# Spectral filter times token mixer: the middle stage's instructions fixed in an order written by hand, and the collecting transfers moved to ScalarE's queue

## The chip, the cores and the metric

The kernel runs on one core of one Trainium2 chip. The metric is the device time of one execution in microseconds (us). The core has a matrix engine (TensorE, PE in the profile, with its weight loads as PEld), VectorE (DVE), ScalarE (ACT), GpSimd (POOL) and SyncE (SP), which here only issues transfers. Transfers issued by SP, ScalarE and GpSimd run on 16 DMA engines that they share. An engine works through its instructions in the order in which the program holds them.

## What is computed

The input x has 2,048 rows (the sequence) of 512 channels. All is float32.

```python
xn = layernorm(x)                                  # over the 512 channels
X  = rfft2(xn, axes=(sequence, channels))          # 2048 x 257, complex
s  = irfft2(X * (w_r + 1j * w_i), s=(2048, 512))   # the spectral filter
h  = layernorm(xn)
u  = gelu(einsum("bsd,sf->bdf", h, w1) + b1)       # mixes along the sequence, F = 1792
y  = einsum("bdf,fs->bds", u, w2) + b2             # and back, w2 is 1792 x 2048
out = x + s * silu(y.transpose(0, 2, 1))
```

## The kernel before

**Two chains of work.** The sequence is laid out as 16 rows `j` of 128 partitions. The filter transforms along the sequence in two steps, along the channels in between, multiplies by the weights, and goes the same way back; all transforms are matrix products with constant tables. The mixer needs products of float32 accuracy from a faster number format: each operand is cut into a high part (a rounded copy, made on ScalarE) and a low part (the difference, on VectorE), and each product is three: high with high, high with low, low with high. A *unit* of the mixer's first product (`hidden`, lines 245 to 250) is three such products of 128x128 by 128x512.

**Stage 1 (lines 350 to 432)** goes over the 16 rows: layer norm, the first seven of the 14 column blocks of w1 in PSUM banks 0 to 6, and the first transform of the filter in bank 7, whose result VectorE folds by symmetry into `ey` (`fold`, line 219).

**Stage 2, the middle stage (lines 435 to 687)**, is where the change lies. It does the other seven column blocks in two batches over 16 rows (`hidden_rest`, 32 parts of w1, 4 units each in the first batch, 3 in the second), and beside them the filter in four *quads* (`filter_quad`). A quad is: 64 products along the channels with `ey` (line 476), four copies to `eys` (478), 64 small products that end the transform along the sequence (485), two copies out of banks 4 to 7 with a swap of neighbouring partitions by two transfers on ScalarE's queue each (`swapped`, 495 to 497), eleven VectorE operations in each of two halves that apply the weights (`weighted`, 512 to 522), 64 small products back (538), and four copies (541). The swapped copies have four buffers, so two halves can be in work. Also in this stage: gelu of finished blocks (line 275, three buffers `u`), and for each pair of blocks the *forms*, the sums and differences that the last stage multiplies, cut in high and low parts (`forms`, 287 to 312). The gelu of a bank must be done before a new block can use the bank. Of w1's low parts, some are made by VectorE (`direct`, line 118), others by a ScalarE copy of the negative and an adding transfer from GpSimd (563 to 567). Weights of the filter are loaded by SP into two buffers, each when the product with the one before it is done (`load_weights`, 438); one of the eight is patched with a second transfer, a GpSimd and a VectorE operation (444 to 447).

**Stage 3 (lines 690 to 900)** multiplies the forms by w2 with a scheme of seven products per pair of rows (`ORDER`, line 692), 21 products of 128x256 each (line 863), whose w2 forms are cut on ScalarE and VectorE (710, 711; three buffers). Beside them the filter's result is taken back along the sequence: `gathered` (781) collects one row of `eys` into a tile `yj` by eight transfers, `sequence` (790) and `channels` (799) transform it, and `finish` multiplies and adds. Tiles of stage 3 (`fin`, line 774) lie where the gelu tiles and the w1 parts of stage 2 lay, and each waits for the ones under it.

**What sets the order.** Most instructions are given to a planner, which orders those of one engine by its own estimate of when each can run. `keep` (line 159) holds the instructions passed through it in the order of the program. In stage 1 nearly all of VectorE's and ScalarE's are kept; in the middle stage only TensorE's products are kept, and VectorE, ScalarE and SP go by the planner. The order of TensorE is a script at the end of the stage (lines 633 to 686), where `products(n)` takes n units and `step(n)` one step of quad n. From line 755 the forms and the w2 forms are kept again for the seam to stage 3.

Of the kernel before, what the change touches and what calls it, by code (L numbers as in the profile page):

```python
# [8 lines left out]
F32 = mybir.dt.float32  # L9
# [99 lines left out]

def spectral_mixer_kernel(tc, x, w1, b1, w2, b2, wk, we, wx, c_f, c_ft, c_d, c_i, c_g, c_h, c_s, out):  # L110
    nc = tc.nc
    V, A, G, T, SY = nc.vector, nc.scalar, nc.gpsimd, nc.tensor, nc.sync
# [12 lines left out]
    with tc.tile_pool(name="ps", bufs=1, space=PSUM) as psp, ExitStack() as left, ExitStack() as right:  # L125
# [32 lines left out]

        keep = tc.keep_in_program_order
# [153 lines left out]

        def form_parts(n, i):
            t, k = form[i][n]
            return t[:, k, :D // 2], t[:, k, D // 2:]
# [56 lines left out]
        of.update({2: (m, 0), 3: (m, 1)})  # L373
        folds = iter(())
        for j in range(NJ):
# [54 lines left out]
            folds = fold(j, first_copy(j, z))  # L430
        run(folds)
        rstage.close()
# [5 lines left out]
        def load_weights(k, i):  # L438
# [4 lines left out]
            if at == ends:  # L443
                SY.dma_start(w[:2, 0], wx[:, 0:3:2])
                one, two = w[:2, 0, 1 - i], w[:2, 0, i]
                G.tensor_sub(one, one, two)
                V.scalar_tensor_tensor(two, two, 2.0, one, op0=ALU.mult, op1=ALU.add)
# [21 lines left out]
        def filter_quad(n, los):  # L469

            gf = mp.tile([P, 4, 32], F32, name=f"gf{n}", tag="gf")
            SY.dma_start(gf, c_g[n].rearrange("p (q c) -> p q c", c=32))
            for q, lo in enumerate(los):
                pd = ps[:, 7 - q]
                for b in range(4):
                    keep(T.matmul(pd[:, b * P:(b + 1) * P], ey[:, lo, b].rearrange("p h j -> p (h j)"), cd[:, b],
                                  start=True, stop=True))
                A.activation(eys[:, lo].rearrange("p (s g c) -> p g s c", s=2, c=64),
                             pd.rearrange("p (g s c) -> p g s c", s=2, c=64), AF.Copy)
                if q % 2:  # L480
                    yield

            for q, lo in enumerate(los):
                for hi in range(4):
                    keep(T.matmul(ps[32 * q:32 * q + 32, 4 + hi], gf[32 * hi:32 * hi + 32, q],
                                  eys[32 * hi:32 * hi + 32, lo], start=True, stop=True))
            hf = mp.tile([P, 4, 2, 32], F32, name=f"hf{n}", tag="hf")
            SY.dma_start(hf, c_h[n].rearrange("p (q s c) -> p q s c", s=2, c=32))
            back, half = [], []

            def swapped(h):
                if not places:
                    place(n)
                e, z = places.pop(0), places.pop(0)
                A.activation(e, ps[:, 4 + 2 * h:6 + 2 * h].rearrange("p b (s c) -> p b s c", s=2), AF.Copy)
                A.dma_start(z[0::2], e[1::2])
                A.dma_start(z[1::2], e[0::2])
                half.append((e, z))

            def weighted(h):  # L500
                at = 4 * n + 2 * h
                e, z = half[h]
                wa, wb = (weights[2 * n + h, i] for i in range(2))
                if at == ends:
                    G.memset(z[:2, 0], 0.0)
                pq = mp.tile([P, 2, 2, 256], F32, name=f"pq{n}_{h}", tag="pq")
                s1 = mp.tile([P, 2, 2, 2], F32, name=f"s1_{n}_{h}", tag="s1")
                er, ei, zr, zi, pr, pi = (a[:, :, s] for a in (e, z, pq) for s in range(2))
                G.tensor_mul(s1[:, 0], z[:, :, :, 0], e1[:, at:at + 2])
                G.tensor_mul(s1[:, 1], e[:, :, :, 0], e2[:, at:at + 2])  # L510
                G.tensor_add(s1[:, 0], s1[:, 0], s1[:, 1])
                V.scalar_tensor_tensor(pr, zi, sg[:, 0:1], er, op0=ALU.mult, op1=ALU.add)
                V.scalar_tensor_tensor(pi, zr, sg[:, 0:1], ei, op0=ALU.mult, op1=ALU.subtract)
# [424 lines left out]
```

## Time and profile before

| | us |
|---|---|
| median of three runs | 416.3 (415.81 to 416.79) |
| the profiled execution | 419.44 |
| its span on the core | 417.4 |
| mean granted TensorE clock in it | 0.963 of full speed |

In the profiled execution the first product of stage 1 on real data starts at 6.8, the first line-476 product of the middle stage at 97.8, the first line-863 product of stage 3 at 223.4. Times of rows count from the start of the span. A view of waits lists, for an engine and line, what released it and for how long it stood; a row of the time order has start, duration, engine, line, operation, `out<-in`, shape, and in square brackets the idle time of the engine ahead of it with what ended it. `SPq` and `ACTq` are the queues in which SP and ScalarE issue transfers. In the chain of waits, each row is a piece of the path followed back from the last instruction: start, length, engine, output tile, line and how many instructions.

### The profile page before, as it was taken

Reading aid. Unit: us, or ns where it says so; the run is one execution under the profiler, and the core shown is the slowest. Engines: PE = TensorE matmul, PEld = TensorE weight load, DVE = VectorE, ACT = ScalarE, POOL = GpSimd, SP = SyncE. Lnnn points to the kernel's source line nnn. Section 1 sums busy time; section 2 is a strip of 40 time slices with the busy share of each in tenths; the row PEclk is TensorE's granted clock in tenths of the full one; section 3 lists DMA queues with packets and bytes.
Section 4 is the critical chain, followed back from the end, with each engine's and each line's share of the span. In section 5 each row is a group of like instructions: output and inputs, shape, how many; then the busy total and the mean of one; then the engine's idle time right before and its main releaser. Section 6 shows DMA issues by size and latency. Waiting matters only on the chain.

```text
span 417.4 us, 7663 instructions
## 1 busy us (share of the span) xinstructions
PE 382.1 (92%) x2760; PEld 336.6 (81%) x2760; DVE 307.4 (74%) x654; ACT 217.0 (52%) x389; POOL 85.9 (21%) x130
## 2 busy tenths in 40 slices
PE   8999999999499799996798589999999998979995
PEld 5888888887287577775577579999999898979994
DVE  5899998773698594969968718767676767664774
ACT  4677755658554545453364724545455444533551
POOL 2133332322141683030000001111111111110200
PEclk9999999999689999999699869999999999999999
DMA  8857384118377998774384489999889999797802
GB/s 266 288 163 244 113 295 156 55 36 236 107 178 191 238 244 258 213 235 133 97 239 90 91 134 195 251 191 213 166 214 197 219 184 202 185 186 168 149 7 53
DMA packets 45298, 73.87 MB, mean 177 GB/s; under 512 B 6388, under 2 KB 28668, under 8 KB 45132
## 3 DMA queue, kind: packets, MB, share of 16 engines
q1 hardware_dynamic: 37228, 55.29, 46.7%
q0 software_dynamic: 6752, 13.90, 20.2%
q10 hardware_dynamic: 1280, 4.20, 2.7%
q8 instruction: 21, 0.34, 0.3%
q14 instruction: 17, 0.14, 0.1%
HBM read 60.78 MB, written 8.13 MB: 165 GB/s over the span
## 4 chain that ended last, share of the span: by engine, by line
PE 60%; DVE 13%; DMA 11%; SPq 5%; ACT 4%; issue 4%; POOL 2%; ACTq 0%; DVEq 0%; POOLq 0%
PE ps L863 22%; PE ps L343 18%; DMA yj<-ey 5%; SPq L784 4%; PE ps L211 3%; PE ps L790 3%; DMA w1s<-in_w_dram 3%; PE ps L248 2%; PE ps L250 2%; DMA w1l<-in_w_dram 2%; PE ps L249 2%; DVE w2f L711 2%; PE ps L799 2%; ACT w2f L710 2%; PE ps L332 1%
## 5 line engine op out<-in xcount | busy, mean ns | idle before, releaser
L343 PE MATMUL ps<-h,w1h 128*128 128x512 f32 x224 | 58.5, 398 | 0.0
L250 PE MATMUL ps<-h,w1l 128*128 128x512 f32 x112 | 45.5, 406 | 9.2 <-DVE w1l L118 6.6
L248 PE MATMUL ps<-h,w1h 128*128 128x512 f32 x112 | 47.0, 419 | 4.1 <-ACT u L275 4.1
L343 PEld LDWEIGHTS ps<-h,w1h 128*128 128x128 f32 x224 | 40.9, 188 | 7.9
L863 PE MATMUL ps<-fa,w2f 128*128 128x256 f32 x336 | 47.0, 296 | 0.0
L711 DVE TENSOR_TENSOR w2f<-s,w2f 128x896 fp32r<-128x896 f32 x32 | 34.8, 1091 | 15.1 <-ACT w2f L710 13.9
L249 PE MATMUL ps<-h,w1h 128*128 128x512 f32 x112 | 45.1, 403 | 0.0
L863 PEld LDWEIGHTS ps<-fa,w2f 128*128 128x128 f32 x336 | 44.3, 203 | 0.0
L863 PE MATMUL ps<-fb,w2f 128*128 128x256 f32 x336 | 43.3, 282 | 0.6 <-DVE c L828 0.6
L863 PE MATMUL ps<-fc,w2f 128*128 128x256 f32 x336 | 41.8, 280 | 0.0
L863 PEld LDWEIGHTS ps<-fb,w2f 128*128 128x128 f32 x336 | 40.8, 188 | 1.2 <-issue 0.8
L863 PEld LDWEIGHTS ps<-fc,w2f 128*128 128x128 f32 x336 | 40.4, 188 | 0.0
L710 ACT ACTIVATE w2f<-s 128x896 fp32r<-128x896 f32 x32 | 30.2, 947 | 15.7 <-DVE s L724 6.4
L711 DVE TENSOR_TENSOR w2f<-a,w2f 128x896 fp32r<-128x896 f32 x24 | 26.1, 1089 | 15.6 <-ACT w2f L710 13.5
L701 POOL DMA_DIRECT2D s<-in_w_dram x16 | 13.6, 852 | 102.3 <-DMA s<-in_w_dram 74.2
L250 PEld LDWEIGHTS ps<-h,w1l 128*128 128x128 f32 x112 | 22.0, 196 | 15.6 <-DVE w1l L118 7.0
L710 ACT ACTIVATE w2f<-a 128x896 fp32r<-128x896 f32 x24 | 22.8, 950 | 21.5 <-PE ps L863 18.7
L248 PEld LDWEIGHTS ps<-h,w1h 128*128 128x128 f32 x112 | 22.0, 196 | 13.9 <-issue 5.0
L343 PE MATMUL ps<-h,w1l 128*128 128x512 f32 x112 | 30.6, 389 | 0.0
L790 PE MATMUL ps<-cft,yj 128*128 128x128 f32 x128 | 18.3, 288 | 11.7 <-DMA yj<-ey 10.1
L834 POOL DMA_DIRECT2D out_dram<-g x15 | 12.8, 856 | 75.6 <-DVE g L832 75.5
L118 ACT ACTIVATE w1h<-w1s 128x384 fp32r<-128x384 f32 (+1 forms) x24 | 13.2, 562 | 26.6 <-DMA w1s<-in_w_dram 16.6
(122 smaller groups left out, 739.6 us busy)
## 6 DMA issues: line engine op xcount, KB each, us to landing
a<-in_w_dram SPq DMA_DIRECT2D x24, 448.0 KB, 4.7
s<-in_w_dram POOLq DMA_DIRECT2D x17, 448.0 KB, 6.9
s<-in_w_dram SPq DMA_DIRECT2D x15, 448.0 KB, 3.9
w1s<-in_w_dram SPq DMA_DIRECT2D x48, 128.0 KB, 3.3
w1r<-in_w_dram SPq DMA_DIRECT2D x16, 256.0 KB, 3.3
wa<-in_wk_dram SPq DMA_DIRECT2D x8, 512.0 KB, 4.1
wb<-in_wk_dram SPq DMA_DIRECT2D x8, 512.0 KB, 5.2
ez<-ez ACTq DMA_DIRECT2D x16, 256.0 KB, 3.6
```

The costliest lines, as they stand in the source:

```text
L118: return A.activation(hi, src, AF.Copy), V.tensor_sub(lo, src, hi.bitcast(F32))
L248: keep(T.matmul(o, w[0][:, sl], hh[j], start=first, stop=False))
L249: keep(T.matmul(o, w[0][:, sl], hl[j], start=False, stop=False))
L250: keep(T.matmul(o, w[1][:, sl], hh[j], start=False, stop=last))
L343: T.matmul(ps[:, bank + i], w[wi][:, i * P:(i + 1) * P], hj, start=first and j == 0, stop=last and j == NJ - 1)
L701: G.dma_start(t, w2_half(*added), accum_op=ALU.add)
L710: ordered(A.activation(wf[:, 0], v, AF.Copy))
L711: ordered(V.tensor_sub(wf[:, 1], v, wf[:, 0].bitcast(F32)))
L784: SY.dma_start(yj[16 * r:16 * r + 16], eys[16 * r + j:16 * r + j + 1])
L790: in_turn(j, T.matmul(pf[:, b], yj[:, b * P:(b + 1) * P], cft, start=True, stop=True))
L834: G.dma_start(out[:, j, cols], g[:, cols], accum_op=ALU.add)
L863: in_turn(j0, T.matmul(o, wf[:, wi, i], ui, start=m + a == 0 and n in (1, 2, 5), stop=m == NH - 1 and a == 2, skip_group_check=n in (6, 3, ...
```

## The change

1. *Program order.* Calls of VectorE, ScalarE, TensorE and SP go through a wrapper `InOrder`. From the second to last row of stage 1 to the end of the middle stage its switch is on, and each of their instructions is kept in the order of the program. GpSimd's stay with the planner.
2. *The order written out.* `filter_quad` is cut into `along_channels`, `turned_in`, `forward`, `swapped`, `weighted` (a generator that yields after each VectorE operation), `way_back` and `turned_back`, and a new script places them among the units: `go(units, ops)` takes units and, spread over them, VectorE operations of the filter. The low part of a w1 part comes one unit behind its high part (`later`). Forms are made by `forms_apart`, whose steps give ScalarE's copies first and VectorE's differences one step later. The next weights are loaded right after the product with the ones before.
3. *The start.* The first three w1 parts are loaded a row ahead, and the first two are cut, between gelus, around the last fold. For the first two rows, the three units of banks 2, 0 and 1 come ahead of those of bank 3.
4. *The collecting transfers* are issued by ScalarE; the first two rows' are placed ahead of stage 3's loop, and a few tiles are allocated ahead of them, so that the `yj` tiles lie further back in the pool. These, and stage 3 as a whole, are not in the fixed order.

The arithmetic is the same. The diff, cut to its core:

```diff
+class InOrder:
+    def __init__(self, engine, keep, switch):
+        self.engine, self.keep, self.switch = engine, keep, switch
+    def __getattr__(self, name):
+        call = getattr(self.engine, name)
+        return (lambda *a, **k: self.keep(call(*a, **k))) if self.switch else call
...
-    V, A, G, T, SY = nc.vector, nc.scalar, nc.gpsimd, nc.tensor, nc.sync
+    keep, fixed = tc.keep_in_program_order, []
+    V, A, T, SY = (InOrder(e, keep, fixed) for e in (nc.vector, nc.scalar, nc.tensor, nc.sync))
+    G = nc.gpsimd
...
+        def forms_apart(i):
...
+            first = (d[0], d[1], u[:, 2]), (a, slice(0, 2), u[:, 0:2])
+            highs(*first)
+            yield
+            lows(*first)
+            V.tensor_sub(u[:, 1], u[:, 1], u[:, 3])
+            V.tensor_sub(u[:, 3], u[:, 2], u[:, 3])
+            V.scalar_tensor_tensor(u[:, 2], u[:, 1], -1.0, u[:, 2], op0=ALU.mult, op1=ALU.subtract)
+            V.scalar_tensor_tensor(u[:, 0], u[:, 2], -1.0, u[:, 0], op0=ALU.mult, op1=ALU.subtract)
...
+            yield
...
+            second = (c, slice(0, 2), u[:, 2:4]), (b, slice(0, 2), u[:, 0:2])
+            highs(*second)
+            yield
+            lows(*second)
             yield
...
             folds = fold(j, first_copy(j, z))
+            if j == NJ - 2:
+                fixed.append(True)
+                for i in range(3):
+                    w1_raw(i)
+        gelu(2, 2)
+        w1_part(0, True, False)
+        gelu(0, 0)
         run(folds)
+        w1_part(1, True, True)
+        gelu(1, 1)
         rstage.close()
...
+                V.scalar_tensor_tensor(pr, zi, sg[:, 0:1], er, op0=ALU.mult, op1=ALU.add)
+                yield
                 V.scalar_tensor_tensor(pi, zr, sg[:, 0:1], ei, op0=ALU.mult, op1=ALU.subtract)
-                V.tensor_mul(pq, pq, wa)
+                yield
+                ends_too(k, 0)
+                V.tensor_mul(pq, pq, weights[k, 0])
+                if k < 7:
+                    load_weights(k + 1, 0)
+                yield
...
+        def next_part(i):
+            if i + 3 < len(parts_):
+                w1_part(i + 3, i % 3 == 0 or i + 3 >= NJ, True)
+            if i + 5 < len(parts_):
+                w1_raw(i + 5)
...
+        def go(units, ops=0):
+            for k in range(units):
                 next(rest)
+                while later:
+                    later.pop(0)()
+                for _ in range((k + 1) * ops // units - k * ops // units):
+                    next(work)
+
+        todo.extend(forms_apart(i) for i in FORMS[:3])
         waiting = [[(3, 3)]]
+        load_tables(0)
+        gelu(9, 6)
+        gelu(8, 5)
+        w1_part(2, True, True)
+        gelu(7, 4)
...
+        go(2)
+        along_channels(0, (3, 2))
+        form_step()
+        turned_in(0, (3, 2))
+        form_step()
+        go(2)
+        along_channels(0, (1, 0))
+        form_step()
+        turned_in(0, (1, 0))
+        form_step()
+        go(1)
+        forward(0)
+        swapped(0, 0)
+        form_step()
+        swapped(0, 1)
+        form_step()
+        load_tables(1)
+        go(3)
...
+        go(11, 12)
+        for n in range(1, 4):
+            if n > 1:
+                go(4, 4)
+                along_channels(n, (0, 1))
+                turned_in(n, (0, 1))
+                go(4, 6)
+                along_channels(n, (2, 3))
+                turned_in(n, (2, 3))
+                go(2, 2)
+            forward(n)
+            swapped(n, 0)
+            go(5, 8)
+            swapped(n, 1)
             form_step()
+            go(2)
             form_step()
+            way_back(n - 1)
...
+            go(1)
+            turned_back(n - 1)
+        for k in range(30):
+            go(1)
+            if k < 24:
+                for _ in range((k + 1) * 5 // 6 - k * 5 // 6):
+                    next(work)
+            if k > 4:
+                form_step()
+        run(work)
+        way_back(3)
+        go(1)
+        turned_back(3)
+        go(2)
+        fixed.clear()
         rstage.close()
...
-                SY.dma_start(yj[16 * r:16 * r + 16], eys[16 * r + j:16 * r + j + 1])
+                A.dma_start(yj[16 * r:16 * r + 16], eys[16 * r + j:16 * r + j + 1])
...
+        made = {"p1_0": fp.tile([P, HD], F32, name="p1_0", tag="p1")}
+        gs = [fp.tile([P, D], F32, name=f"g{j}", tag="g", bufs=2) for j in (0, NP)]
+        made["c11_0"] = fp.tile([P, HD], F32, name="c11_0", tag="c", bufs=2)
+        ya, yb = gathered(0), gathered(NP)
         for p in range(NP):
...
-                if k == 0 and p == 0:
-                    ya, yb = gathered(j0), gathered(j1)
```

More of the change, by code (lines that the diff above doesn't have):

```diff
@@ L506, in weighted, with swapped @@
+        def swapped(n, h):
+            if not places:
+                place(n)
+            e, z = half[n, h] = places.pop(0), places.pop(0)
+            A.activation(e, ps[:, 4 + 2 * h:6 + 2 * h].rearrange("p b (s c) -> p b s c", s=2), AF.Copy)
+            A.dma_start(z[0::2], e[1::2])
+            A.dma_start(z[1::2], e[0::2])
+        def weighted(n):
+            for h in range(2):
+                at, k = 4 * n + 2 * h, 2 * n + h
+                e, z = half[n, h]
                 pq = mp.tile([P, 2, 2, 256], F32, name=f"pq{n}_{h}", tag="pq")
@@ new lines, in unit @@
+        def unit(i, k, bank):
+            j = parts_[i][0]
+            hidden(j, k, bank, parts[i])
+        def next_part(i):
[3 more added lines that the diff above has]
+                w1_raw(i + 5)
+            if i >= NJ:
+                passed[0] = i - NJ + 1
+        def hidden_rest():
+            first, second = BATCHES[0][1], BATCHES[1][1]
+            for i in range(2):
+                for k, bank in first[:3]:
+                    unit(i, k, bank)
+                    yield
+            for i in range(2):
+                unit(i, *first[3])
+                next_part(i)
+                yield
+            for i in range(2, NJ):
+                for k, bank in first:
+                    unit(i, k, bank)
+                    if i == NJ - 1 and k != 1:
+                        gelu(*{2: (10, 0), 3: (11, 1), 0: (4, 3)}[k])
+                    if k == 0:
+                        next_part(i)
+                    yield
+            todo.extend([forms_apart(3), forms_apart(4)])
+            waiting.append([(5, 2)])
+            for i in range(NJ, 2 * NJ - LATE // 3):
+                for k, bank in second:
+                    unit(i, k, bank)
+                    if k == 0:
+                        next_part(i)
+                    yield
+            w1_part(2 * NJ - 1, True, False)
@@ L621, in hidden_rest @@
                 gelu(ft, bank)
-        chain = [filter_quad(n, los) for n, los in enumerate(QUADS)]
         rest = hidden_rest()
-        def products(n):
-            for _ in range(n):
+        work = (None for n in range(4) for _ in weighted(n))
+        def go(units, ops=0):
+            for k in range(units):
                 next(rest)
-        def step(n):
-            next(chain[n])
-        for ft, bank in ((9, 6), (8, 5), (7, 4)):
-            gelu(ft, bank)
-        todo.extend(forms(i) for i in FORMS[:3])
```

255 lines of the change are left out of this document (106 added, 149 removed).

## The prediction

> **What bounds the kernel now.** I read the page first, then the chain of waits, TensorE's busy time and granted clock by stretches of the middle stage, and TensorE's waits.
>
> ```profile
> PE 382.1 (92%) x2760; PEld 336.6 (81%) x2760; DVE 307.4 (74%) x654; ACT 217.0 (52%) x389; POOL 85.9 (21%) x130
> 49.49 4.80 PE ps L343 x21
> 169.94 1.78 PE ps L476 x16
> 175.14 1.20 PE ps L485 x30
> 212.43 1.42 PE ps L538 x61
> 291.74 6.66 PE ps L863 x55
> ```
>
> TensorE is busy for 92% of the span, but busy is not full speed. The five chain rows give its pace when nothing stops it: 4.80 / 21 = 0.229 us per 512-wide product, 1.78 / 16 = 0.111 per 128-wide one, 0.040 and 0.023 for the small ones, and 6.66 / 55 = 0.121 per 256-wide product of the final stage. The first stage runs at that pace throughout. The middle stage holds 112 units of three products (76.9 us), 8 x 1.78 = 14.2 of transforms along the channels, 128 x 0.040 = 5.1 and 256 x 0.023 = 5.9: 102 us. It lasts from 97.8 to about 223.4, which is 125.6, so some 23 us are lost there.
>
> ```profile
> 105.60:117.80 12.20, 6.46 (x23) 5.41 (x23) 8.28 (x16) 7.02 (x11) 4.34 (x6) 0.58 0.47 134
> 194.70:206.50 11.80, 5.24 (x13) 4.13 (x13) 11.80 (x22) 1.80 (x4) 0.62 (x1) 0.71 0.35 104
> 206.50:223.40 16.90, 16.90 (x132) 13.31 (x131) 12.13 (x21) 11.04 (x20) 1.70 (x2) 1.00 0.71 187
> 223.40:250.30 26.90, 19.09 (x133) 18.19 (x132) 15.10 (x25) 12.11 (x20) 0.84 (x1) 0.81 0.60 113
> 250.30:413.00 162.70, 156.25 (x1304) 154.14 (x1302) 113.24 (x229) 76.74 (x129) 23.93 (x28) 0.99 0.81 176
> 370.00:380.00 10.00, 7.86 (x54) 7.65 (x53) 5.97 (x12) 3.29 (x5) 0.86 (x1) 0.83 0.95 209
> ```
> ```profile
> PE ps L250 <- DVE w1l L118: 6.6, 1, 6.6
> PE ps L790 <- DMA yj<-ey: 6.4, 1, 6.4
> PE ps L248 <- ACT u L275: 4.1, 2, 3.8
> PE ps L250 <- DMA w1l<-in_w_dram: 2.5, 2, 2.2
> PE ps L476 <- ACT ez L495: 1.9, 1, 1.9
> PE ps L863 <- ACT fd L280: 1.2, 1, 1.2
> ```
>
> The columns of the stretches are length, busy time of TensorE, its weight loads, VectorE, ScalarE and GpSimd, then granted clock, DMA share and GB/s. Each large wait is followed by a low clock: it costs twice. In 105.6 to 117.8 the work at full pace is two units and one set of 16, 1.37 + 1.78 = 3.2, so 9.0 are lost; in 194.7 to 206.5 it is 13 x 0.229 = 3.0, so 8.8 are lost. The wait for a transfer takes 2.4. Those three are 20 of the 23. From 223.4 to 250.3, where the final stage starts, the work is 24 x 0.111 + 109 x 0.121 = 15.9, so 11.0 are lost, the 6.4 for the collecting transfers and its slow clock first. From 250.3 on, 232 x 0.111 + 1,072 x 0.121 = 155.5 of 162.7: 7 lost.
>
> **Part by part. The start of the stage.** The order written by hand puts the first low part of w1 ahead of the last row's fold on VectorE, and two ScalarE activations ahead of that.
>
> ```profile
> 96.93 0.69 ACT L275 ACTIVATE u<-ps,b1t 128x512 f32<-128x512 f32 x1
> 97.98 0.63 ACT L118 ACTIVATE w1h<-w1s 128x512 fp32r<-128x512 f32 x1
> 95.65 0.43 DVE L221 TENSOR_TENSOR o<-zt 128x256 f32<-128x256 f32 x1 [1.62 <-ACT zt L216]
> 97.99 0.60 DVE L232 SCALAR_TENSOR_TENSOR ey<-t,o 128x128 f32<-128x128 f32 x2 [0.78 <-ACT o L229]
> 98.64 0.69 DVE L118 TENSOR_TENSOR w1l<-w1s,w1h 128x512 fp32r<-128x512 f32 x1
> ```
>
> Before, the fold ran from 95.65 to 98.59, 2.9 long. Now: gelu ends at 97.6, the high part 0.63 later, the low part 0.69 after that, at 98.9; the fold ends at 101.8. TensorE has two units for this time (to 99.9) and waits 1.9. In return the bank that gelu(3, 3) must clear, the 3.8 us wait above, is asked for as the seventh unit and not the fourth.
>
> ```profile
> L495 ACT ACTIVATE ez<-ps 128x1024 f32<-128x1024 f32 x8 | 8.2, 1023 | 4.4 <-DVE pq L522 1.9 <-PE ps L485 1.7 <-ACT w1h L563 0.6
> ```
>
> I follow ScalarE from there, at 0.6 to 0.7 an activation of 512. The fold's own small copy, which waits for VectorE, ends near 100.8; two w1 parts and four gelus take it to 104.6, the first form's high parts to 105.5, two transform copies to 106.6. The second high parts wait for the low parts and four operations of VectorE, until 107.6, and end at 108.8; two more copies at 109.9. TensorE stands ahead of the first `forward` from 107.4: 2.5. That takes 1.3, the copy of 1.0 and two issues of 0.55 bring ScalarE to 113.3, gelu(3, 3) to 114.0; TensorE has one unit meanwhile and waits 2.1. So 1.9 + 2.5 + 2.1 = 6.5 of waits stand against 9.0 lost: 2.5 gained, if the clock holds.
>
> ```profile
> 139.39 0.47 PE L250 MATMUL ps<-h,w1l 128*128 128x512 f32 x1 [2.19 <-DMA w1l<-in_w_dram]
> 372.56 1.16 PE L790 MATMUL ps<-cft,yj 128*128 128x128 f32 x8 [2.14 <-DMA yj<-ey]
> ```
>
> A wait of 3.8 lost the clock, one of 2.19 did not (the stretches around it are at 1.00), one of 2.14 did: 0.83 over ten microseconds, 1.7 us. My three waits could thus cost three times 1.7 more: the bounds of this part are a gain of 2.5 and a loss of 2.6. I take 2.5, since units lie between them. The Trainium skill, TensorE: Matmul & The Clock Gate, section Why this matters for your kernels, says that gaps over some 3 us lose the clock; by it the 2.5 would be sure. The 372.56 row speaks against it.
>
> **The body of the middle stage.** The 6.6 wait comes from VectorE's order: it was busy for all 11.80 of that stretch, with filter operations that stood ahead of a low part of w1. Now the low part follows one unit later, so that wait goes. What is late next is VectorE itself.
>
> ```profile
> 114.52 0.76 DVE L512 SCALAR_TENSOR_TENSOR pq<-ez,sg,ez 128x512 f32<-128x512 f32 x1 [3.44 <-DMA ez<-ez]
> L514 DVE TENSOR_TENSOR pq<-pq,wa 128x1024 f32<-128x1024 f32 x8 | 9.7, 1213 | 0.0
> L512 DVE SCALAR_TENSOR_TENSOR pq<-ez,sg,ez 128x512 f32<-128x512 f32 x8 | 6.0, 744 | 5.5 <-DMA ez<-ez 3.4 <-PE ps L538 2.1
> L519 DVE TENSOR_TENSOR ez<-ez 128x512 f32<-128x512 f32 x8 | 5.5, 682 | 0.0
> L118 DVE TENSOR_TENSOR w1l<-w1s,w1h 128x384 fp32r<-128x384 f32 x16 | 8.8, 553 | 6.2 <-ACT w1h L118 6.2
> L300 DVE TENSOR_TENSOR u<-u 128x256 f32<-128x256 f32 x7 | 3.0, 424 | 0.2
> ```
>
> One half of the filter is 2 x 1.21 + 4 x 0.74 + 4 x 0.68 + 0.2 = 8.3, or 7.6 as operations overlap by some 0.07; a quad 15.2. A form is near 4.0 (four of 0.42, and low parts of 0.69 and less). In the new order the first filter operation stands behind the forms of two tiles and starts at about 121, by my walk, where it started at 114.5. It then needs 15.2 a quad beside 18 units, 12.3, plus 3.6 + 1.3 + 1.5 of transforms on TensorE, 18.7. So TensorE sets the pace for quads 2 and 3, after one wait at the first `way_back`: with 0.6 for a low part VectorE ends the first quad at 121 + 15.8 = 136.8; only then is a buffer free for the next copy of 1.0, to 137.8, and TensorE is there at 135.2: 2.6. The last quad's filter starts near 175, and in its 24 units lie 15.2 + 3.9 of w1 parts + 10 of forms = 29 of VectorE against 16.5 of TensorE. The last way back then comes at about 206; the chain row above has it at 212.4. That is 6.4 for start and body together, so about 3.5 to 4 for the body; I take 3.5. Bounds: 8.8 + 2.4 gained, if VectorE never holds TensorE; 4 lost, if the later start, 6.5, is not made good. On SP the second wk load and its wx patch hold the w1 loads behind them, as they did before; the GpSimd work between is unmoved and may keep the 2.2 wait, which I don't count as a gain.
>
> **The collecting transfers at the seam.**
>
> ```profile
> SPq L699 <- DVE fb L281: 9.5, 1, 9.5
> 234.18 10.06 SPq L784 DMA_DIRECT2D yj<-ey  x16
> yj<-ey SPq DMA_DIRECT2D x128, 32.0 KB, 4.3
> 158.51 0.47 ACTq L496 DMA_DIRECT2D ez<-ez  x1
> 159.02 0.62 ACTq L497 DMA_DIRECT2D ez<-ez  x1
> 159.77 0.63 ACT L564 ACTIVATE w1l<-w1h 128x512 fp32r<-128x512 f32 x1 [0.77 <-ACT w1h L563]
> L710 ACT ACTIVATE w2f<-s 128x896 fp32r<-128x896 f32 x32 | 30.2, 947 | 15.7 <-DVE s L724 6.4 <-PE ps L863 6.1 <-DVE s L734 3.0
> L711 DVE TENSOR_TENSOR w2f<-s,w2f 128x896 fp32r<-128x896 f32 x32 | 34.8, 1091 | 15.1 <-ACT w2f L710 13.9
> ```
>
> SP stood 9.5 us at a w2 load that waits for the last form, and the sixteen issues, 0.63 apart, were queued behind it. On ScalarE they are not, and by the new allocation order their tiles no longer lie over the gelu tiles; they can be issued at the end of the middle stage, 20 us before use. The wait of 6.4 and its slow clock go, some 10 of the 11. The cost is 16 x 0.63 = 10.1 of ScalarE's queue, where it is busy 11.0 of 16.9 and 12.1 of 26.9: between 0 (all in its idle time) and 10. I take 3, nearer to 0, as most of its time is idle. Net gain 7, bounds 0 and 10.
>
> **The steady final stage.** Per pair of rows TensorE needs 147 x 0.121 + 32 x 0.111 = 21.3. ScalarE is busy 76.7 in 162.7, 10 a pair, and gets 16 issues more, 10.1: together 20. An issue runs beside the activation before it; two in a row held the next one by 0.77. If eight go in one block, 5.0, and a w2 form can be late by two products less its own two steps (0.95 on ScalarE, 1.09 on VectorE), 5.1 - 2.0 = 3, the block costs 2.0; fourteen blocks, 28. Dealt out between activations they cost 0. I take 0.5 each, 7, nearer to 0, since ScalarE is idle half the time. An issue that must wait for a free tile now holds the copies and w2 forms behind it on ScalarE, and TensorE behind those; on SP only loads stood behind it. The gain is nearly all of the 7 lost there, as transfers no longer stand behind w2 loads; these loads come earlier too and share the DMA engines (0.81 busy) with them. Net 0, bounds +7 and -21.
>
> Sum: 2.5 + 3.5 + 7 + 0 = 13. The profiled execution took 419.4 (span 417.4 and 2.0 around it); 406.4 against it, and against the median of 416.3, 3.1 below it, 403.3.
>
> **The rivals.** *ScalarE becomes the bound of the final stage* (slower). The gains without its cost are 2.5 + 3.5 + 7 + 7 = 20. A block that costs over 20 / 14 = 1.4 eats them; at the full 2.0 the time is 416.3 - 20 + 28 = 424. For it: 20 of 21.3 is full in an engine that must also wait. Against: its deadlines are two products off. *VectorE is the bound of the middle*: its filter starts 6.5 later and nothing makes it up, middle gain 0, time 416.3 - 7 = 409. *New waits lose the clock*: the start loses 2.6, the body 4, the seam brings 7: 416. *All that is lost comes back*: start 2.5, the body's upper bound of 11, seam 10, final stage 7: 386, and anything below 394 counts as this. *The transfer, not its queue, is late*: landing takes 4.3 with the DMA engines at 0.81 to 0.95, so the 6.4 stays and ScalarE pays 3 besides: 416.3 - 6 + 3 = 413. That last one is near a rule of the Trainium skill, DMA: Bandwidth & Descriptors, section Issuing engines are not separate DMA queues: another issuing engine saves only issue time, usually small beside the transfer. Here eight issues, 5.0, are longer than 4.3.
>
> **How the numbers follow.** Forecast (398 to 408) 0.37, VectorE-bound 0.17, late transfers 0.06, all back 0.08: faster 0.68. ScalarE-bound 0.23 and half of the lost clock 0.05: slower 0.28; the other half, 0.04, within 0.2% (0.8 us, about what a measurement of this kernel can tell from none). The range is 394 to 424: 0.08 lies below it, some 0.1 above.
>
> **What would show it.** Right: no wait above 2.5 in 98 to 118, first filter operation near 121, last L538 near 206, first L790 by 232 with no wait for yj, and clock 1.00 through the seam. Wrong: ScalarE rows with idle time put down to issue in blocks of 4 to 5 us, and L863 waiting on w2f (the slower rival); w1l waits after 180 (VectorE); yj waits that stay (the transfer).

## The result, and the profile after it

The changed kernel takes 463.4 us, the median of four runs (459.8 to 468.6), where the kernel before takes 416.6 beside it: a ratio of 1.110, 95% interval 1.103 to 1.117. It is 47 us slower. The forecast was 403, with a range of 394 to 424. The profiled execution took 459.8, its span is 458.0. Times here and below are medians of all runs of a kernel; the ratios leave out executions that took some per cent longer at a lower granted clock.

The page's engine row, and the stretches of the changed kernel that answer to those of before (length, busy time of TensorE, its weight loads, VectorE, ScalarE and GpSimd, granted clock, DMA share, GB/s):

```profile
PE 391.6 (85%) x2760; PEld 337.5 (74%) x2760; DVE 311.0 (68%) x654; ACT 215.1 (47%) x389; POOL 77.9 (17%) x130
```
```profile
90.00:121.00 31.00, 25.97 (x154) 19.79 (x153) 15.59 (x33) 19.25 (x34) 6.84 (x17) 0.94 0.38 120
121.00:180.40 59.40, 52.67 (x417) 39.67 (x415) 45.28 (x64) 25.98 (x44) 15.99 (x22) 0.94 0.82 216
180.40:227.90 47.50, 35.91 (x276) 24.07 (x275) 36.99 (x63) 15.50 (x29) 3.42 (x7) 0.93 0.38 118
227.90:245.66 17.76, 13.45 (x46) 9.63 (x47) 11.59 (x19) 10.12 (x18) 1.70 (x2) 0.81 0.73 189
245.66:275.00 29.34, 14.16 (x99) 13.77 (x98) 9.03 (x15) 8.43 (x15) 1.68 (x2) 0.71 0.63 118
275.00:453.00 178.00, 159.89 (x1330) 157.10 (x1330) 115.64 (x233) 78.62 (x135) 23.25 (x27) 0.99 0.75 155
```

No engine has become a bound. In the last quad's stretch, 180.4 to 227.9, VectorE is busy for 37.0 of 47.5 and ScalarE for 15.5, and TensorE still stands. At the seam, 245.7 to 275.0, each of the three is busy for less than half of the time. So what costs must be waits, and not the amount of work. TensorE's waits:

```profile
PE ps L969 <- ACT p L924: 15.2, 2, 14.3
PE ps L894 <- DMA yj<-ey: 8.2, 4, 3.0
PE ps L118 <- DVE pq L118: 7.5, 4, 2.3
PE ps L894 <- issue: 6.2, 3, 3.5
PE ps L118 <- ACT w1h L118: 4.5, 3, 3.0
PE ps L259 <- ACT w1h L442: 3.0, 1, 3.0
PE ps L118 <- DMA w1l<-in_w_dram: 3.0, 1, 3.0
```

(Line 118 is now the wrapper, so all calls in program order carry it; tiles tell them apart. Line 969 is 863 of before, 894 is 790, 888 the collecting issue.) The 6.6 us wait for a low part of w1 made by VectorE is gone, as forecast (two waits of that kind are left, 1.4 together); the one for a transfer into `w1l` is not. The largest wait is new: 14.3 us for the copy of `p1`, which ScalarE makes of the first result of stage 3. ScalarE in order of time says why:

```profile
136.50 1.00 ACT L118 ACTIVATE ez<-ps 128x1024 f32<-128x1024 f32 x1
139.84 1.12 ACTq L118 DMA_DIRECT2D ez<-ez  x2
141.01 0.42 ACT L118 ACTIVATE fd<-u 128x256 fp32r<-128x256 f32 x1 [3.50 <-DMA wa<-in_wx_dram]
...
203.86 0.63 ACT L118 ACTIVATE fc<-u 128x512 fp32r<-128x512 f32 x1 [4.62 <-DVE u L118]
...
214.24 0.63 ACT L118 ACTIVATE fc<-u 128x512 fp32r<-128x512 f32 x1 [3.87 <-DVE u L118]
...
228.85 0.63 ACT L118 ACTIVATE fc<-u 128x512 fp32r<-128x512 f32 x1 [9.28 <-DVE u L118]
...
251.89 15.15 ACTq L888 DMA_DIRECT2D yj<-ey  x13
267.08 0.39 ACT L924 ACTIVATE p<-ps 128x256 f32<-128x256 f32 x1 [15.05 <-DMA yj<-ey]
```

Thirteen collecting issues in a row take 15.15 us, 1.17 each, where sixteen on SP took 10.06 before, 0.63 each; and the p1 copy stands behind them, released by collecting transfers, not by its data. After that it goes on in blocks: the activations of `g`, `w2f` and `p` stand 66.9 us (29.4 + 18.8 + 18.7) behind collecting transfers in the whole run:

```profile
ACT g L928 <- DMA yj<-ey: 29.4, 7, 5.8
ACT fc L118 <- DVE u L118: 18.9, 4, 9.3
ACT w2f L814 <- DMA yj<-ey: 18.8, 8, 3.2
ACT p L924 <- DMA yj<-ey: 18.7, 2, 15.1
```

The middle rows of ScalarE's order show the other loss: the form parts `fc` stand 4.6, 3.9 and 9.3 us for operations of VectorE, which in the program stand behind the filter's, and everything that ScalarE does later stands with them. VectorE in its turn waits for ScalarE:

```profile
DVE w2f L815 <- ACT w2f L814: 48.7, 23, 6.2
DVE w1l L118 <- ACT w1h L118: 28.0, 14, 5.7
```

The second row is 28.0 us at low parts whose high part is late. So the profile splits the loss in two. Stage 3's first line-969 product is at 245.66 where it was at 223.44: 22.2 lost by then. From there to the end of the span it takes 212.3, where it took 194.0: 18.3 more. The same two numbers are given for each experiment below.

### The profile page after: what moved, and what is told of

The parts are those of the page before. It is cut to its first block, busy times and chain, and to the rows that moved or that the text cites. A ratio compares the mean times of both kernels' runs of the same rounds, so it can differ in the third digit from the quotient of the medians.

```text
span 458.0 us, 7656 instructions
## 1 busy us (share of the span) xinstructions
PE 391.6 (85%) x2760; PEld 337.5 (74%) x2760; DVE 311.0 (68%) x654; ACT 215.1 (47%) x389; POOL 77.9 (17%) x130
## 3 DMA queue, kind: packets, MB, share of 16 engines
q0 software_dynamic: 6752, 13.90, 18.3%
## 4 chain that ended last, share of the span: by engine, by line
PE 46%; DMA 19%; DVE 15%; ACT 9%; issue 5%; ACTq 5%; SPq 0%; POOL 0%; DVEq 0%; POOLq 0%
PE ps L393 16%; DMA yj<-ey 14%; PE ps L969 12%; PE ps L118 10%; ACTq L888 4%; DVE pq L118 4%; PE ps L222 3%; DVE ez L118 3%; PE ps L894 2%; ACT w2f L814 2%; PE ps L903 2%; DVE w2f L815 2%; DMA s<-in_w_dram 1%; PE ps L382 1%; DMA w1l<-in_w_dram 1%
## 5 line engine op out<-in xcount | busy, mean ns | idle before, releaser
L118 PE MATMUL ps<-h,w1h 128*128 128x512 f32 x214 | 71.2, 418 | 6.8 <-ACT w1h L118 4.5
L969 PE MATMUL ps<-fc,w2f 128*128 128x256 f32 x336 | 45.2, 290 | 14.3 <-ACT p L924 14.3
L118 PEld LDWEIGHTS ps<-h,w1h 128*128 128x128 f32 x214 | 40.7, 199 | 22.1 <-issue 5.8
L393 PE MATMUL ps<-h,w1h 128*128 128x512 f32 x210 | 54.9, 398 | 0.0
L969 PEld LDWEIGHTS ps<-fc,w2f 128*128 128x128 f32 x336 | 42.6, 197 | 14.7 <-ACT p L924 14.5
L815 DVE TENSOR_TENSOR w2f<-s,w2f 128x896 fp32r<-128x896 f32 x32 | 34.7, 1090 | 19.1 <-ACT w2f L814 18.8
L118 PE MATMUL ps<-h,w1l 128*128 128x512 f32 x107 | 43.7, 416 | 4.4 <-DMA w1l<-in_w_dram 3.0
L969 PE MATMUL ps<-fa,w2f 128*128 128x256 f32 x336 | 45.9, 290 | 0.9 <-ACT p L924 0.9
L393 PEld LDWEIGHTS ps<-h,w1h 128*128 128x128 f32 x210 | 38.4, 188 | 7.4
L969 PEld LDWEIGHTS ps<-fa,w2f 128*128 128x128 f32 x336 | 42.4, 195 | 1.3 <-ACT p L924 1.2
L814 ACT ACTIVATE w2f<-s 128x896 fp32r<-128x896 f32 x32 | 30.1, 947 | 25.1 <-DMA yj<-ey 18.8
L118 DVE TENSOR_TENSOR w1l<-w1s,w1h 128x384 fp32r<-128x384 f32 (+1 forms) x23 | 13.8, 605 | 28.0 <-ACT w1h L118 28.0
L894 PE MATMUL ps<-cft,yj 128*128 128x128 f32 x128 | 18.4, 281 | 14.3 <-DMA yj<-ey 8.2
L928 ACT ACTIVATE g<-c,b2t 128x256 f32<-128x256 f32 x24 | 12.2, 506 | 38.4 <-DMA yj<-ey 29.4
L118 PEld LDWEIGHTS ps<-h,w1l 128*128 128x128 f32 x107 | 21.2, 198 | 11.2 <-DMA w1l<-in_w_dram 3.4
L393 PE MATMUL ps<-h,w1l 128*128 128x512 f32 x105 | 28.7, 389 | 0.0
L894 PEld LDWEIGHTS ps<-cft,yj 128*128 128x128 f32 x128 | 16.2, 193 | 15.6 <-issue 15.6
```

What stands on the lines that cost most here:

```text
L118: return (lambda *a, **k: self.keep(call(*a, **k))) if self.switch else call
L393: T.matmul(ps[:, bank + i], w[wi][:, i * P:(i + 1) * P], hj, start=first and j == 0, stop=last and j == NJ - 1)
L814: ordered(A.activation(wf[:, 0], v, AF.Copy))
L815: ordered(V.tensor_sub(wf[:, 1], v, wf[:, 0].bitcast(F32)))
L894: in_turn(j, T.matmul(pf[:, b], yj[:, b * P:(b + 1) * P], cft, start=True, stop=True))
L928: A.activation(g[:, cols], src, AF.Silu, bias=b2t[:, j:j + 1], scale=scale)
```

## The experiments

The theories. **B**: the collecting issues hold ScalarE, and so the seam and stage 3. **A**: in the middle it is the fixed order of VectorE, ScalarE and SP that costs, not the new script of TensorE. Rivals: the transfers themselves are late; the script's later filter sets the pace; one engine alone is to blame. "First product" is the start of stage 3's first product in the profiled execution, "rest" the span from there.

| kernel | us | before beside it | ratio, 95% | first product | rest |
|---|---|---|---|---|---|
| before | | | | 223.4 | 194.0 |
| the change | 463.4 | 416.6 | 1.110, 1.103 to 1.117 | 245.7 | 212.3 |
| a_gsp | 438.2 | 415.6 | 1.055, 1.046 to 1.065 | 248.4 | 189.7 |
| b_alloc | 416.0 | 415.6 | 1.002, 0.997 to 1.006 | 222.4 | 192.2 |
| b_alloc_gact | 445.0 | 415.6 | 1.069, 1.058 to 1.080 | 222.4 | 220.5 |
| a_gsp_tonly | 413.8 | 415.6 | 0.996, 0.992 to 0.999 | 219.1 | 193.8 |
| a_one_A | 424.3 | 416.2 | 1.020, 1.012 to 1.027 | 244.5 | 177.2 |
| a_two_A | 443.5 | 416.7 | 1.070, 1.062 to 1.079 | 247.5 | 191.9 |
| a_four_A | 455.2 | 414.6 | 1.095, 1.088 to 1.102 | 239.8 | 210.2 |
| a_gsp_vfree | 421.0 | 416.2 | 1.015, 1.005 to 1.025 | 226.1 | 192.5 |
| a_gsp_afree | 418.6 | 416.2 | 1.006, 1.002 to 1.009 | 230.4 | 188.0 |
| a_gsp_spfree | 431.1 | 416.2 | 1.032, 1.023 to 1.041 | 236.8 | 188.9 |
| a_gsp_vonly | 420.8 | 416.7 | 1.009, 1.005 to 1.013 | 225.8 | 191.2 |
| a_gsp_aonly | 423.1 | 416.7 | 1.016, 1.010 to 1.022 | 231.2 | 190.8 |
| a_one_later | 422.3 | 416.7 | 1.016, 1.009 to 1.023 | 238.7 | 179.8 |
| a_one_swapsp | 420.7 | 417.7 | 1.005, 1.000 to 1.009 | 242.3 | 175.6 |
| b_one_A | 402.8 | 414.6 | 0.971, 0.968 to 0.974 | 222.1 | 179.1 |
| b_one_SY | 405.9 | 414.6 | 0.978, 0.974 to 0.983 | 221.7 | 182.8 |
| t_one_A | 400.6 | 414.6 | 0.964, 0.959 to 0.969 | 219.5 | 182.0 |
| t_one_direct | 397.4 | 417.7 | 0.952, 0.947 to 0.957 | 214.2 | 179.4 |

The kernels with the unchanged fixed middle (the change, a_gsp, a_one_A, a_two_A, a_four_A) have their first product between 239.8 and 248.4 although that stage is the same in all: a single profile of it scatters by 9 us, and differences of first products below that say little.

### The two parts apart

**a_gsp**, the change with SP collecting again:

```diff
-                A.dma_start(yj[16 * r:16 * r + 16], eys[16 * r + j:16 * r + j + 1])
+                SY.dma_start(yj[16 * r:16 * r + 16], eys[16 * r + j:16 * r + j + 1])
```

> The changed kernel with its collecting transfers given back to SP, everything else kept. Theory B (the seam and the final stage lost 18.3 us because ScalarE stands in its collecting issues: 15.15 us for thirteen of them, then 3 to 6 us a block): the final stage goes back to about 194 us from its first product, the 15 us wait of L924 goes, about 445. Rival (the collecting transfers are late whichever queue holds them, since the middle ends late and w2 loads are in the way): no more than 5 us come back, 458 or above.

438.2: 25 us came back, more than theory B's 18, and the rest of the span, 189.7, is below that of before; the rival, late transfers whichever queue holds them, allowed 5. SP still stood at the w2 load ahead of the sixteen issues, as before:

```profile
246.43 10.28 SPq L803 DMA_DIRECT2D a<-in_w_dram  x2
256.75 0.43 SPq L883 DMA_DIRECT2D xr<-in_x_dram  x1
257.23 10.06 SPq L888 DMA_DIRECT2D yj<-ey  x16
```

**b_alloc_gact** and **b_alloc**, the kernel before with this part alone (the `made`, `gs` and `ya, yb` lines of the diff), issued by ScalarE and by SP:

> The kernel before with only the last part of the change: the new allocation order, both first rows collected ahead of the products, and the collecting transfers on ScalarE. The middle stage is untouched. Theory B: about 18 us lost, 431 to 437, with a long row of collecting issues on ScalarE ahead of the p1 copy. Rival (the loss belongs to the hand-ordered middle alone and the move is as good as predicted): 416 or below, down to 406.

> The kernel before with the new allocation order and both first rows collected ahead of the products, but the issues stay on SP. Theory B: the order of allocation costs nothing, and SP still stands 9.5 us at the w2 load that waits for the last form, so 414 to 417.5. Rival (the allocation order itself is what hurts the seam): 425 or above.

On an untouched middle the move costs 29 us, and the new allocation order with SP's issues costs nothing. That is theory B, which had expected some 18. The new order of allocation is cleared; eight issues a row on ScalarE's queue are not. ScalarE at the seam of b_alloc_gact:

```profile
231.38 14.97 ACTq L784 DMA_DIRECT2D yj<-ey  x13
246.40 0.38 ACT L820 ACTIVATE p<-ps 128x256 f32<-128x256 f32 x1 [14.88 <-DMA yj<-ey]
```

**a_gsp_tonly**, a_gsp with only TensorE kept in program order:

```diff
-    V, A, T, SY = (InOrder(e, keep, fixed) for e in (nc.vector, nc.scalar, nc.tensor, nc.sync))
+    T = InOrder(nc.tensor, keep, fixed)
+    V, A, SY = nc.vector, nc.scalar, nc.sync
```

> The changed kernel with collecting on SP and only TensorE held to program order in the middle stage; VectorE, ScalarE and SP are left to the planner. Theory A (the middle lost 22 us because these three, each held in order, wait for one another): at least 15 of them come back, 423 to 431 against 445 for the same kernel with all four held. Rival (the script itself, the order of TensorE's units and the later filter, sets the pace): within 4 us of the same kernel with all four held.

413.8, 24 us less than a_gsp and slightly less than before: theory A, which asked for 15 or more. The script of TensorE, the later filter and the earlier w1 parts are all in this kernel; with SP collecting and only TensorE fixed they are a gain of 0.4% (interval 0.1 to 0.8). VectorE's 28.0 us at late high parts are 6.2 here:

```profile
DVE w1l L445 <- ACT w1h L443: 6.2, 3, 4.2
```

These are two steps of one chain, 463.4 to 438.2 to 413.8, so their sum proves nothing. The check is each part by itself against the kernel before: 29 for the move (b_alloc_gact) and 22.6 for the fixed order (a_gsp) make 52, where both together cost 47. The intervals are 3 to 5 us to either side, so as far as they tell the two parts are separate.

### What about the collecting transfers costs

**a_one_A**, the change with each row collected in one transfer in place of eight:

```diff
-            for r in range(8):
-                A.dma_start(yj[16 * r:16 * r + 16], eys[16 * r + j:16 * r + j + 1])
+            A.dma_start(yj, eys[j::16])
```

> The changed kernel, still collecting from ScalarE, but each row in one transfer of 256 KB where it was eight of 32 KB: the same bytes, one issue for eight. Theory B1 (ScalarE is held because of the number of issues: beyond the first few, each waits until an earlier transfer has landed): the 15 us row at the seam goes and so do the blocks after it; 463 comes down to 436 to 442, what the same kernel gets with its eight issues on SP. Rival B2 (a transfer issued from ScalarE is in the way by itself, or the bytes are late): 455 or above.

424.3: 39 us came back, 14 more than by giving the issues to SP, and more than theory B1 had expected (436 to 442). ScalarE's queue is the wrong place for eight issues a row, and not for one. The same on the kernel before, from ScalarE (**b_one_A**) and from SP (**b_one_SY**):

> The kernel before, middle stage untouched, with the new allocation order and each row collected by ScalarE in one transfer of 256 KB. The same with eight transfers a row took 445, with eight on SP 416. Theory B1 (only the number of issues costs; the benefits that were forecast for the move, 7 at the seam and 7 after it, are there): 397 to 404. Rival (the gain of the changed kernel from one transfer came from its slower middle, and there is nothing to gain here): 413 or above.

> The same with the one transfer a row on SP, behind the w2 load that waits 9.5 us for the last form. Theory B1 with the engine of some worth: two issues of 0.6 stand where sixteen took 10, but the 9.5 us stay, so 403 to 411, above the kernel that collects from ScalarE. Rival (the count is everything, the engine nothing): within 2 us of it.

402.8 and 405.9. With b_alloc and b_alloc_gact these are the four corners: eight transfers a row from SP 416.0, from ScalarE 445.0; one a row from SP 405.9, from ScalarE 402.8. One transfer a row is worth 10 on SP and 42 on ScalarE, and only then is ScalarE the better queue, by 3 (the intervals of the two ratios just touch). The pieces themselves, eight small ones in place of one, thus cost 10 where SP issues them; the other 32 belong to ScalarE as the issuer. The p1 copy in b_one_A is no longer held by transfers:

```profile
228.66 1.17 ACTq L783 DMA_DIRECT2D yj<-ey  x1
229.86 0.64 ACTq L783 DMA_DIRECT2D yj<-ey  x1
...
231.42 0.38 ACT L819 ACTIVATE p<-ps 128x256 f32<-128x256 f32 x1 [0.71 <-DVE fb L281]
```

Why an issue waits can be read in the program's own list of ScalarE's instructions, for the change and then for a_one_A (line, transfer, what it waits for):

```
L888 DMA yj0_2544<-ey_71 16x1x512 x3
L888 DMA yj0_2544<-ey_71 16x1x512 [waits DMAHW0_49]
...
L887 DMA yj0_2544<-ey_71 128x1x512
L887 DMA yj8_2546<-ey_71 128x1x512
```

In this program the transfers of SP and ScalarE signal their end on eight counters (`DMAHW0` to `DMAHW7`), used in turn. An issue whose counter is still owed an earlier transfer waits for that transfer to land. Of the first sixteen issues thirteen carry such a wait, seven for an earlier collecting transfer and six for a load that SP issued. With one transfer a row the first two carry none.

**a_four_A** and **a_two_A** collect a row in four and in two (the diff is that of a_two_A; a_four_A steps by 2):

```diff
-            for r in range(8):
-                A.dma_start(yj[16 * r:16 * r + 16], eys[16 * r + j:16 * r + j + 1])
+            for r in range(0, 8, 4):
+                A.dma_start(yj[16 * r:16 * r + 64], eys[16 * r + j:16 * r + j + 49:16])
```

> The changed kernel with four transfers of 64 KB a row from ScalarE, where it had eight of 32 and the other run one of 256. Theory B1, that an issue beyond the first few waits until an earlier transfer lands: eight issues in place of sixteen at the seam, most of the wait of 15 us goes but not all, 428 to 445, between 424 and 463. Rival (only very many issues hurt): 426 or below; the other rival (the small size of the pieces, not their count): 450 or above.

> The changed kernel with two transfers of 128 KB a row from ScalarE. One a row took 424, four 455, eight 463; at the seam the p1 copy stood 0, 8.7 and 15.1 us behind sixteen, eight and two issues' worth of waits (0 for two issues, 8.7 for eight, 15.1 for sixteen). Theory (an issue waits for an earlier transfer only when too many are under way; four at the seam are few enough): the p1 copy stands under 2 us, 424 to 432. Rival (every issue beyond one a row costs, by an even price from 424 to 455 over three more transfers a row): about 434 to 440. Other rival (the size of the pieces does it, 128 KB in 64 partitions is as bad): 445 or above.

Both came out worse than theory B1 expected, 455.2 and 443.5. The first lies in the range of the rival that the size of the pieces does it (450 or above), the second between two rivals' ranges. The seam went as the count has it: the p1 copy stood 15.05 us behind sixteen issues, 8.68 behind eight, and 3.59 behind four, where the list has one issue that waits.

```profile
247.56 8.70 ACTq L888 DMA_DIRECT2D yj<-ey  x6
256.30 0.38 ACT L924 ACTIVATE p<-ps 128x256 f32<-128x256 f32 x1 [8.68 <-DMA yj<-ey]
```
```profile
254.00 3.86 ACTq L888 DMA_DIRECT2D yj<-ey  x2
257.90 0.39 ACT L924 ACTIVATE p<-ps 128x256 f32<-128x256 f32 x1 [3.59 <-issue]
```

But there is no knee at a few issues: by the medians the three doublings, from one to eight, cost 19, 12 and 8; the rests are 177, 192, 210 and 212. With two a row it is a few waits of TensorE, for the p1 copy and for `yj`, that a_one_A has not (there 0.9 and none), and some slow clock after them (0.93 in 277.5 to 327.5):

```profile
PE ps L969 <- ACT p L924: 7.6, 3, 3.2
PE ps L894 <- DMA yj<-ey: 5.8, 2, 3.9
```

With four, ScalarE stands for 32.1 us (21.8 + 10.3) behind collecting transfers, half of the 66.9 with eight, and another 17.5 behind output transfers, a wait that the change doesn't have; why these are late there stays open.

```profile
ACT g L928 <- DMA out_dram<-g: 17.5, 5, 5.9
```

That the price lies in small packets is excluded by the queue rows of the change, a_four_A and a_one_A (queue: packets, MB, share of the 16 engines):

```profile
q10 hardware_dynamic: 5376, 8.40, 11.4%
```
```profile
q10 hardware_dynamic: 3456, 8.39, 5.1%
```
```profile
q10 hardware_dynamic: 3456, 8.39, 6.0%
```

Eight transfers a row make more and smaller packets, but four a row make the same as one, and cost 31 us more. That it lies in pieces of a few partitions is not excluded by these rows, but SP's own eight pieces cost 10 and not 42. The Trainium skill, DMA: Bandwidth & Descriptors, section Rules for kernel authors, advises one 128-partition transfer in place of two to disjoint partition halves; 443.5 against 424.3 agrees, here with the issuing engine's own work as the victim. The same section of the Trainium skill says that one pays mostly overhead under 64 KB. Here 64 and 128 KB, issued from ScalarE, still cost 31 and 19 us more than 256 KB.

### Which engine's order costs

**a_gsp_vfree**, **a_gsp_afree** and **a_gsp_spfree** release one engine of a_gsp from program order (the `InOrder` line without it); **a_gsp_vonly** and **a_gsp_aonly** hold one beside TensorE.

> The changed kernel with collecting on SP, and VectorE left to the planner in the middle stage; ScalarE, SP and TensorE held in order. 438 with all held, 414 with TensorE alone held. Theory A1 (it is VectorE standing in order that matters, 29.5 us at low parts whose high part is late): 15 or more back, 423 or below. Theory A2 (ScalarE): less than 9 back, 429 or above. Theory A3 (SP): the same, 429 or above.

> The same with ScalarE left to the planner, and VectorE, SP and TensorE held. Theory A2 (ScalarE standing in order at swaps, at form parts that wait for VectorE (18.5 us) and at copies, holds the high parts that VectorE and TensorE wait for): 12 or more back, 426 or below. Theories A1 and A3: 430 or above. I hold A2 the likeliest, with A1 behind it.

> The same with SP left to the planner, and VectorE, ScalarE and TensorE held. Theory A3 (SP's loads of w1 stand behind wk loads that wait for the filter, so high parts are late): 12 or more back, 426 or below. Theories A1 and A2: within 5 us of 438.

> The changed kernel with collecting on SP; in the middle stage TensorE and VectorE held in order, ScalarE and SP left to the planner. TensorE alone held took 414, all four 438. Theory (a ring: it takes two held engines that wait for one another): 412 to 418. Rival (VectorE's order costs by itself): 422 or above.

> The same with TensorE and ScalarE held, VectorE and SP left to the planner. Theory (a ring): 412 to 419. Rival (ScalarE's order costs by itself): 422 or above.

| held beside TensorE | none | V | A | V, SP | A, SP | V, A | V, A, SP |
|---|---|---|---|---|---|---|---|
| us | 413.8 | 420.8 | 423.1 | 418.6 | 421.0 | 431.1 | 438.2 |

Releasing VectorE and releasing ScalarE each gave what its own theory had asked for, A1 and A2, so neither engine alone is to blame; SP's 431.1 fits none of the three. The ring, by which one held engine costs nothing, falls for ScalarE (423.1, in the rival's range); for VectorE 420.8 lies between the two ranges. VectorE's order alone costs 7 us, ScalarE's 9, both 17, which is about the sum. SP's order costs 7 beside both and nothing beside one (418.6 and 421.0 against 420.8 and 423.1), so that part does need more than one held engine. It also goes when ScalarE or VectorE is released from all three, which gives 20 or 17.

Two links were tried with all held. **a_one_swapsp** issues the swaps' transfers from SP (`A.dma_start(z...` to `SY.dma_start(z...`), **a_one_later** puts two more `yield` ahead of `highs(*second)` from the third form on.

> The changed kernel with one collecting transfer a row from ScalarE (424.3), all four engines held, and the swap's transfers issued from SP in place of ScalarE. Theory (ScalarE is held some 3.5 us at three swaps by their issue): 415 to 421. Rival (the same wait moves to SP and holds the w1 loads there, or the filter's input comes later): 423 or above.

> The changed kernel with one transfer a row from ScalarE (424), all four engines held, and one link loosened: from the third form on, ScalarE's second high parts come two steps later, so that they stand behind the next high part of w1 and not ahead of it. ScalarE stood 18.5 us in four such waits for VectorE. Theory (ring): part of that comes back, 418 to 422. Rival (VectorE is simply full there, and the forms now come later): 424 or above.

420.7 against 424.3 for a_one_A: the ratios, 1.005 (to 1.009) and 1.020 (from 1.012), stand apart, so the swaps' issues on ScalarE are a link, worth 3.5 us by the medians and 6 by the ratios. It is the 136.50 row above: the copy ends at 137.5, its transfers are issued at 139.84, and nothing on ScalarE moves until the patch `wx` has landed. The swap doesn't read the patch. By the program's list its first issue waits, among others, for the counter of SP's load of `wa`, and its second for that of the patch: the counters at work again, as at the seam. 422.3 for a_one_later is inconclusive: its interval and that of a_one_A overlap for the most part.

### Both repairs

**t_one_A** is a_gsp_tonly with one collecting transfer a row from ScalarE. **t_one_direct** has every low part of w1 from VectorE besides:

```diff
-                w1_part(i + 3, i % 3 == 0 or i + 3 >= NJ, True)
+                w1_part(i + 3, True, True)
```

> The changed kernel with only TensorE held in order in the middle stage and each row collected by ScalarE in one transfer. If the two losses are separate and both repairs add: 413.8 less the same 15 to 19, 394 to 399. Rival (they overlap): 405 or above.

> TensorE alone held, one collecting transfer a row from ScalarE (400.6), and every low part of w1 made by VectorE; the eight adding transfers of GpSimd (5.6 us from issue to landing) are gone, and VectorE has eight subtractions of 0.69 more, 5.5. Theory (those transfers are the last wait of the middle, 7.8 us): 393 to 398. Rival (VectorE is full there, and takes the place): 399 to 404.

400.6 (a little above what was expected) and 397.4 (as expected), a ratio of 0.952: 20 us faster than before. The wait that t_one_A had left,

```profile
PE ps L118 <- DMA w1l<-in_w_dram: 7.8, 2, 5.4
```

is gone from the last kernel, and VectorE had room for the eight subtractions. Its engine row:

```profile
PE 377.8 (96%) x2760; PEld 332.6 (84%) x2760; DVE 311.9 (79%) x662; ACT 210.8 (54%) x381; POOL 91.9 (23%) x122
```

## Why the prediction was wrong, point by point

**The start: the waits right, the gain smaller.** First filter operation of VectorE forecast near 121, found at 120.55; waits forecast 1.9, 2.5 and 2.1, found 0.9 (two pieces), 1.74 and 2.27. They cost some clock, 0.94 in 90 to 121: after the wait of 2.27 products took 0.63. By 121.7 the changed kernel has done 12 units, 48 products along the channels and one `forward`, 14.9 us at the prediction's paces; by 121.6 before had done 8 units, 64 products and one `forward`, 13.9. So the gain is some 0.8 where 2.5 was forecast: an estimate from the rows of TensorE, and within the bounds.

**The body: wrong.** Start and body were to bring 6; the first product of stage 3 came 22.2 later, so they were 28 off together, nearly all of it in the body. Forecast was a gain of 3.5 for the body with VectorE's work as the next bound and the last way back at 206. It came at 224.4, and VectorE was idle for 10.5 of the last 47.5 us. The step that failed is the sentence that TensorE sets the pace for quads 2 and 3: it set VectorE's 15.2 of work against TensorE's 18.7 as if each could do its work whenever it had time. With the planner that was nearly so (a_gsp_tonly is 1.8 us faster than before, of the 6 forecast). In program order it is not: an operation that isn't ready holds all behind it, on each of three engines, and the walk through their orders was made for the start alone. The `wx` patch was named as holding the w1 loads "as they did before"; what was missed is that in the fixed order the swap's issue waits for it, on ScalarE, by a counter.

**The seam and stage 3: the price wrong.** Gains were put at 10 at the seam (7 and the 3 of cost) and 7 after it, 17. b_one_A, which has the move with two issues a pair, runs the rest in 179.1 where before took 194.0: 14.9. That is near, but not for the reason given alone: b_one_SY, where SP still issues, has 11.2 of it. The price of the issues was put at 3 + 7 = 10, bounds 0 and 38. b_alloc_gact against b_one_A, same first product, has it at 220.5 - 179.1 = 41.4. The two side by side, from their first products on:

```profile
222.36:252.36 30.00, 13.63 (x90) 13.02 (x89) 11.79 (x20) 7.56 (x12) 0.84 (x1) 0.72 0.67 135
```
```profile
222.13:235.13 13.00, 11.38 (x92) 10.77 (x91) 11.07 (x19) 6.96 (x11) 0.00 (x0) 1.00 0.45 113
```

b_alloc_gact needs 30 us for the 90 products that b_one_A does in 13. So two terms are mis-sized: the 3 at the seam is some 17, outside its bounds of 0 and 10, and "I take 0.5 each" is some 24 / 14 = 1.7, near the 2.0 of the slower rival. The reason is in the working: an issue was priced at its length, 0.6, from SP's rows, and the thirteen at the seam took 1.17 each, as they wait for landings. Of issues waiting for a free tile the prediction spoke; not of waiting for a counter. The order at the seam was also taken for granted: the issues could go "20 us before use", but the stage after the script is ordered by the planner, which put them right ahead of the p1 copy.

**The rivals.** ScalarE holding stage 3 was given 0.23 and 424; by sign and engine it is what happened to that half (445 by itself). Its path was another: the rival had w2 forms late, but none of TensorE's waits after 245.66 is for a w2 form; the largest are for the p1 copy (15.2) and at the products that take `yj` (8.2 for its transfer and 6.2 that the view puts down to issue). That the middle would lose was seen only as lost clock, 416. The late transfers, given 0.06, are out as a cause: with SP issuing 25 us came back. The Trainium skill, DMA: Bandwidth & Descriptors, section Issuing engines are not separate DMA queues, has issue time as usually small beside the transfer. One issue at the seam took 1.17 us and a collecting transfer of the change landed 3.6 us after its issue (median), which agrees; but thirteen issues in a row, 15.15, were not small.

**What would show it wrong** was listed and came in part: ScalarE stood in issues, and waits for `yj` stayed, though they were listed for late transfers and here come from late issues. TensorE waiting on w2 forms did not come. The w1l waits after 180 that were listed for VectorE came to 1.4 us only; the high parts came late, from ScalarE.

## What to carry to other kernels

Price an issue on a compute engine by the landing of the transfer that last used its counter, not by its own length, and merge transfers before moving them: here one in place of eight was worth 10 us on SP and 42 on ScalarE. Fixing one engine's order by hand needs a walk through that engine's whole queue, DMA issues included; fixing three at once cost 24 us here, and the same script with TensorE alone fixed was no slower than before. What stays open is how VectorE's and ScalarE's 7 and 9 us divide among their single waits: of the links, only the swaps' issues were shown. Why four transfers a row cost nearly as much as eight after the seam is open too.

## What the runs showed of the hardware

Two waits of TensorE of the same length, 2.98 us, had different effects in the changed kernel:

```profile
215.86 0.73 PE L118 MATMUL ps<-h,w1h 128*128 128x512 f32 x2 [2.98 <-ACT w1h L118]
...
237.31 0.79 PE L259 MATMUL ps<-h,w1h 128*128 128x512 f32 x1 [2.98 <-ACT w1h L442]
237.90 0.63 PE L260 MATMUL ps<-h,w1h 128*128 128x512 f32 x1
```
```profile
215.00:225.00 10.00, 7.70 (x43) 4.93 (x43) 9.29 (x14) 2.99 (x7) 0.00 (x0) 1.00 0.20 59
...
235.00:245.00 10.00, 7.69 (x25) 6.13 (x26) 5.99 (x10) 3.69 (x6) 0.83 (x1) 0.66 0.60 123
```

After the first the clock stayed at 1.00, after the second it was 0.66 over ten microseconds, with products of 0.63 for the usual 0.39. Shorter waits stood ahead of both, 1.32 of the first and 0.98 of the second, so these do not tell them apart. At the start of the stage a wait of 2.27 lost the clock as well. The Trainium skill, TensorE: Matmul & The Clock Gate, section Why this matters for your kernels, puts the limit at gaps of some 3 us. Here waits below it, from 2.1 to 3.0, went either way, so a forecast should not count on a wait just below it being harmless.
